# Loads, copies and a bank pool re-arranged at two stage boundaries of a recurrent-attention training kernel

## The chip, the cores and the metric

The kernel runs on one core of one Trainium2 chip. The metric is the device time of one launch in microseconds (us), lower being better. TensorE (PE) multiplies matrices and also transposes 128x128 blocks, VectorE (DVE) and ScalarE (ACT) copy results from PSUM to SBUF and do elementwise work, GpSimd (POOL) does small SBUF copies and issues some transfers, and SyncE (SP) issues most transfers. Each engine works through its own instructions strictly in order.

## The reference, cut to what matters

The output is the forward value and all gradients of `x + A(xn) + B(xn)`, where `xn` is the layer norm of `x` (2048 rows of 512, bf16).

```python
# A: attention over 64 segments of 32 rows; 8 memory rows are carried from segment to segment
for s in range(64):
    h = concat([mem, xn[32*s : 32*s+32]])            # 40 rows
    q, k, v = h @ Wq, h @ Wk, h @ Wv                 # 32 heads of 128
    p = softmax(mask(q @ k.T * 128**-0.5))
    o = (p @ v) @ Wo                                 # summed over heads
    mem, out[s] = o[:8], o[8:]
# B: the dense part
r = relu(xn @ w1 + b1);  B = (r * r) @ w2 + b2       # 512 -> 1792 -> 512
_out, _vjp = jax.vjp(_f, x, mem0, Wq, Wk, Wv, Wo, w1, b1, w2, b2)
return _out, *_vjp(grad_out)
```

## The kernel before, in words

The program has four stages.

1. The first stage (pool `pp`, planner `BIAS_0`) does the layer norm and the dense part in eight blocks of 256 rows. At its start it loads `B_w1` and `B_w2` in seven pieces of 256 KB each (`CUT`), the first blocks of `x` (`ln_in`) and of `grad_out` (`gN0`), and `b1`. It transposes the gradient block (`ps_gT`), the normalised block (`ps_xT`, `ln`) and the weights (`turn_w`: `ps_W2T`, `ps_W1T`) on TensorE, and runs `mlp_a(0)` (`ps_h`), `mlp_b(0)`, and so on.
2. The forward recurrence (pool `pc`, eight PSUM banks `c0` to `c7`) runs `chain(s)` for segments 0 to 63, with work off the chain in between (`l_proj`, `l_attn`, `dw_unit`). At its end `turn` transposes half of Wv on TensorE (`ps_Wv`), and `turn_o` transposes Wo in place inside the tile `WB` (`ps_Wo`): 16 groups of eight 128x128 blocks, each group read back by two copies of 512 elements per partition.
3. The backward recurrence runs `chain(s)` for segments 63 to 0 in a second set of PSUM banks (pool `pc2`, banks `c0` to `c6` and `r0`) and a second set of SBUF tiles (pool `bw`, opened after the forward's pool `fw` is closed). It begins with the remaining 40 groups of transposes of Wv, Wk and Wq (`ps_Wv`, `ps_Wk`, `ps_Wq`) and with the first loads (`l_pre`, `load`). In `chain`, `proj("c", "gO", ...)` multiplies the incoming gradient with the transposed Wo into two banks `ps_gO`, each is copied to a half of the tile `gN` (named `gON` in the profile), and from there transposed again (`ps_gOT`) and multiplied on. `l_pre` does the same for the memory rows (`gL`).
4. The last stage forms the weight gradients of the attention (`ps_gw`).

Within stages 1 to 3 the order of the instructions on every engine is written out by `_Plan.run`. Each piece of work is added with an estimated cost for each engine that may do it and, for a transfer, a time `lat` until it lands. The planner picks greedily by earliest start and by rank, where the rank is the longest estimated path to the end plus a fixed table `BIAS`, and also decides whether DVE or ACT does a copy. The chip does not re-order: if something arrives later than the plan has it, the engine and all that is queued behind it wait. Every `run()` of the kernel before starts from time 0 on all engines and all banks. At the start of the backward's plan a pseudo operation `A({"X": 8.0}, ..., ["WB"])` holds back, in the plan alone, what reads WB.

The Wo rows arrive in an interleaved order, so the old copy in `turn_o` picks every 128th element of PSUM to write a plain row of 128 (`"p j (a c) -> p j a c"` on the SBUF side). Everything behind it sees heads in their natural order.

Of the kernel before, what the change touches and what calls it, by code (L numbers as in the profile page):

```python
# [78 lines left out]
BF16 = mybir.dt.bfloat16  # L79
# [18 lines left out]
def pe(cost, shape, n=8):  # L98
    x = _PE(PE=cost)
    x.shape = shape  # L100
    x.n = n
    return x
# [6 lines left out]
class _Plan:  # L109
# [199 lines left out]
def kernel(  # L309
# [148 lines left out]
    class Stage:  # L458
# [38 lines left out]
        def turn_o(self, kind, nm, reg, key, okey, lift=0.0):  # L497

            for g in range(2 * NI):
                i, d0 = g // 2, 2 * (g % 2)  # L500
                blk = reg.rearrange("p (i c d) -> p i c d", i=NI, c=JQ)[:, i]
                bk = self.bank(kind, [P, 2, JQ, P], BF16, "ps_" + nm)

                def tr(e, blk=blk, bk=bk, d0=d0):
                    for d in range(2):
                        for c in range(JQ):
                            transpose_to(bk()[:, d, c, :], blk[:, c, (d0 + d) * P:(d0 + d + 1) * P])
                self.plan.add(pe(0.46, "f"), tr, [key] if g else [], [bk] + ([] if g else [key]), 1, lift=lift)
                for d in range(2):
                    self.evict(lambda blk=blk, d=d0 + d: blk[:, :, d * P:(d + 1) * P].rearrange("p j (a c) -> p j a c", c=JQ), bk,  # L510
                               lambda bk=bk, d=d: bk()[:, d].rearrange("p c (j a) -> p j a c", j=JQ), [(okey, g, d)], 1, {"DVE": 0.61, "ACT": 0.59})

        def sq_T(self, src, sk, dst, dk, prio):

# [15 lines left out]
        def proj(self, kind, nm, win, wkeys, Wt, col0, dst, prio):  # L530
            for half in range(2):
                bk = self.bank(kind, [P, 512], F32, "ps_" + nm)
                for dq in range(2):
                    def mm(e, half=half, dq=dq, bk=bk):
                        for dc in (2 * dq, 2 * dq + 1):
                            for j in range(JQ):
                                c0 = col0 + j * HW + half * 512
                                nc.tensor.matmul(  # L538
                                    bk()[32 * j:32 * (j + 1), :], lhsT=win(dc), rhs=Wt(dc, c0),
                                    start=(dc == 0), stop=(dc == DC - 1), tile_position=(0, 32 * j),  # L540
                                )
# [37 lines left out]
        def mixed(self, nm, pre, terms, rkeys, dst, prio, lift=0.0):  # L579

            bks = [self.bank("d", [P, 512], F32, "ps_" + nm) for _ in range(2)]
            for half in range(2):
                bk = bks[half]

                def mm0(e, half=half, bk=bk):
                    for k in range(4):
                        for x, (lf, rf) in enumerate(pre):
                            nc.tensor.matmul(bk()[:, k * P:(k + 1) * P], lhsT=lf(4 * half + k), rhs=rf(4 * half + k),  # L588
                                             start=(k == 0 and x == 0), stop=False, skip_group_check=True)
                self.plan.add(pe(0.22 * len(pre), "f", 4 * len(pre)), mm0, rkeys[0](half), [bk], prio, lift=lift)  # L590
            for half in range(2):
                bk = bks[half]

                def mm(e, half=half, bk=bk):
                    for k in range(4):
                        i = 4 * half + k
                        for x, (lf, rf) in enumerate(terms):
                            for j in range(JQ):
# [3 lines left out]
                self.plan.add(pe(0.222 * len(terms), "d", 16 * len(terms)), mm, rkeys[1](half), [bk], prio)  # L602
# [94 lines left out]
    with tc.tile_pool(name="p0", bufs=1) as p0, \  # L697
# [4 lines left out]
        def tl(name, shape, dt=BF16):  # L702
            return p0.tile(shape, dt, name=name)
# [179 lines left out]
        for g in range(NRB):  # L883
            if g == 0:
                ln_in(0)
                for h, (f0, f1) in enumerate(CUT):
                    sg.dma(lambda f0=f0, f1=f1: W1[:, :, P * f0:P * f1],
                           lambda f0=f0, f1=f1: B_w1.rearrange("(c p) f -> p c f", p=P)[:, :, P * f0:P * f1], [], [("W1", h)], lat=6.0)
                    if h == 1:
                        sg.dma(lambda: gN0, lambda: pair(gflat, 0), [], ["gxb"], lat=6.0)  # L890
                        sg.dma(lambda: b1Tb[:], lambda: B_b1.rearrange("(c p) -> p c", p=P), [], ["b1Tb"], lat=5.0)
                    sg.dma(lambda f0=f0, f1=f1: W2[:, f0:f1, :],
                           lambda f0=f0, f1=f1: B_w2.rearrange("(c p) d -> p c d", p=P)[:, f0:f1, :], [], [("W2", h)], lat=8.0)
                sg.dma(lambda: b2r[:], lambda: B_b2.rearrange("(o n) -> o n", o=1), [], ["b2r"], lat=5.0)
                A({"DVE": 0.1}, lambda e: V.tensor_copy(b1T[:], b1Tb[:]), ["b1Tb"], ["b1T"])
                ln(0)
                bk = sg.bank("B", [P, DC, RB], BF16, "ps_gT")

                def trg(e, bk=bk):
                    for k in range(2):  # L900
                        for dc in range(DC):
                            transpose_to(bk()[:, dc, k * P:(k + 1) * P], gN0[:, k, dc * P:(dc + 1) * P])
                A({"PE": 0.5}, trg, ["gxb"], [bk])
                A({"DVE": 0.7, "ACT": 1.05}, lambda e, bk=bk: ev({"DVE": "v", "ACT": "s"}[e], gTb[0], bk()[:]), [bk], [("gT", 0)])
                for u in range(FC // 2):
                    turn_w(u, "W2T")
                ln_in(1)
                ln_in(2)
                ln(1)
# [30 lines left out]
                   lat=8.0, cost=0.6, eng="POOL")  # L940
        plan.run()

    with tc.tile_pool(name="fw", bufs=1) as fw, \
            tc.tile_pool(name="pc", bufs=1, space=bass.MemoryType.PSUM) as pc:
        PLp = []
        for v in range(SPB):
            t_ = fw.tile([P, NI, RL], BF16, name="PLp%d" % v)
# [342 lines left out]
        l_attn(TC - 1)  # L1290
        sg.turn("m", "Wv", Wqkv[2], ("WA", 2), "WvT", 0, 8)
        sg.turn_o("c", "Wo", WB[:], "WB", "WoT", 40.0)
        plan.run()

    bw_cm = tc.tile_pool(name="bw", bufs=1)
    bw = bw_cm.__enter__()
    pc2_cm = tc.tile_pool(name="pc2", bufs=1, space=bass.MemoryType.PSUM)
    pc = pc2_cm.__enter__()
    if True:
        def tl(name, shape, dt=BF16):  # L1300
            return bw.tile(shape, dt, name=name)
# [39 lines left out]

        plan = _Plan(tc, PAR[2], BIAS[2])
        S7 = [("c", x) for x in range(7)]
        sg = Stage(plan, pc, {"c": (4, S7), "f": (1, S7), "l": (1, S7), "e": (1, S7), "w": (4, S7), "r": (1, [("r", 0)]), "d": (3, S7), "t": (3, S7)})
        A = plan.add
        V = nc.vector
        LKIND = "r"
# [248 lines left out]
        for y in range(NEARLY):  # L1596
# [2 lines left out]
                    nc.tensor.matmul(pw0[k]()[:], lhsT=HNc[:, RCS[y], k * P:(k + 1) * P], rhs=gbuf[y][:, 0:512],  # L1599
                                     start=(y == 0), stop=False)  # L1600
            A(pe(0.86, "f", 4), mm0, [("gn", y), ("HN", RCS[y] // BPC), "gNat"], pw0)
        plan.run()
    bw_cm.__exit__(None, None, None)

    with tc.tile_pool(name="p5b", bufs=1) as p5b, tc.tile_pool(name="p5e", bufs=1) as cs1, \
# [60 lines left out]
        with tc.manual_schedule():  # L1666
            load_gn(0)
            for x in range(4 * JQ):
# [4 lines left out]
                if x == 2 * JQ:  # L1673
# [3 lines left out]
                gns = gq.pop(x)  # L1677
                bks = [(lambda b=b: b()[:]) for b in (
                    (pw0 if x == 0 else [sg.bank("w", [P, 512], F32, "ps_gw", b.key) for b in pw0])
                    + [sg.bank("w", [P, 512], F32, "ps_gw", k) for k in S7 + [("r", 0)] if k not in [b.key for b in pw0]])]  # L1680
# [25 lines left out]
    pc2_cm.__exit__(None, None, None)  # L1706
    fww_cm.__exit__(None, None, None)


# [33 lines left out]
```

## Time and profile before

| what | value |
|---|---|
| three timed runs | 2806.7 us median, 2800.26 to 2809.99 |
| profiled execution, first to last instruction | 2798.3 us |
| busy share PE / DVE / ACT / POOL | 95% / 47% / 35% / 29% |
| PE busy in 0 to 30 us | 18.25 us |
| PE busy in 30 to 250 us | 215.52 of 220 us |
| PE busy in 1186 to 1236 us (end of forward, start of backward) | 43.49 of 50 us |
| PE busy in 1236 to 2200 us (backward) | 926.36 of 964 us |

The profiled execution is one launch. Its own time is given only as its span from the first to the last instruction, which is 8.4 us under the median of the timed runs and 2.0 us under the lowest of them. A stage's worth is read from the idle time of TensorE in it. A bracket at the end of a row of the timeline is the time that the engine stood idle before that instruction, and behind the arrow is what ended it.

### The profile page before, as it was taken

Reading aid. Unit: us, or ns where it says so; the run is one execution under the profiler, and the core shown is the slowest. Engines: PE = TensorE matmul, PEld = TensorE weight load, DVE = VectorE, ACT = ScalarE, POOL = GpSimd, SP = SyncE. Lnnn points to the kernel's source line nnn. Section 1 sums busy time; section 2 is a strip of 40 time slices with the busy share of each in tenths; the row PEclk is TensorE's granted clock in tenths of the full one; section 3 lists DMA queues with packets and bytes.
Section 4 is the critical chain, followed back from the end, with each engine's and each line's share of the span. In section 5 each row is a group of like instructions: output and inputs, shape, how many; then the busy total and the mean of one; then the engine's idle time right before and its main releaser. Section 6 shows DMA issues by size and latency. Waiting matters only on the chain.

```text
span 2798.3 us, 125071 instructions
## 1 busy us (share of the span) xinstructions
PE 2664.6 (95%) x54888; PEld 1538.5 (55%) x55072; DVE 1327.3 (47%) x3327; ACT 985.8 (35%) x2012; POOL 824.8 (29%) x2431
## 2 busy tenths in 40 slices
PE   8998999999999999999999999999999899999999
PEld 6664555555555555575555555555555444444444
DVE  5544455555455555565455455555455402232322
ACT  4333444444444444364444444444444300000000
POOL 1111111111111111145555555555555301112210
PEclk9999999999999999999999999999999999999999
DMA  6657656555557566647777676777766698788861
GB/s 211 202 172 205 180 160 175 164 166 163 156 169 186 169 185 175 177 118 178 187 181 187 179 189 179 189 192 190 188 182 177 201 344 273 232 255 270 257 185 42
DMA packets 499792, 530.91 MB, mean 190 GB/s; under 512 B 223845, under 2 KB 325398, under 8 KB 497070
## 3 DMA queue, kind: packets, MB, share of 16 engines
q1 hardware_dynamic: 480254, 463.06, 59.9%
q0 software_dynamic: 15056, 53.56, 5.6%
q8 instruction: 430, 7.05, 1.1%
q10 hardware_dynamic: 3936, 6.29, 0.7%
q14 instruction: 116, 0.95, 0.1%
HBM read 249.77 MB, written 237.52 MB: 174 GB/s over the span
## 4 chain that ended last, share of the span: by engine, by line
PE 45%; DVE 4%; issue 3%; DMA 3%; ACT 1%; POOL 1%; SPq 0%; DVEq 0%; ACTq 0%; POOLq 0%
PE ps_gw L1690 14%; PE ps_dRA L1370 8%; PE ps_gw L1694 5%; PE ps_gO L538 3%; PE ps_dRL L1370 3%; PE ps_d L624 2%; DMA dLN<-S_GNL 2%; PE ps_d L573 1%; PE ps_d L599 1%; PE ps_gOT L429 1%; PE ps_d L588 1%; PE ps_gm L1524 1%; PE ps_gL L538 1%; PE ps_dL L1481 1%; PE ps_dP L1468 1%
## 5 line engine op out<-in xcount | busy, mean ns | idle before, releaser
L1370 PE MATMUL ps_dRA<-WA,dT 128*32 128x512 bf16 x6144 | 377.0, 381 | 5.3 <-issue 2.5
L1690 PE MATMUL ps_gw<-WA,WB 128*128 128x512 bf16 x1505 | 330.6, 379 | 1.6
L1690 PEld LDWEIGHTS <-WB 128*128 128x128 bf16 x1896 | 185.4, 98 | 225.0 <-issue 1.7
L538 PEld LDWEIGHTS <-PA 128*32 128x32 bf16 x8192 | 195.4, 96 | 192.3 <-DVE PA L1190 22.3
L435 ACT CAST dN<-ps_d 128x512 bf16<-128x512 f32 x372 | 207.4, 590 | 184.7 <-PE ps_d L599 112.3
L1370 PEld LDWEIGHTS <-dT 128*32 128x32 bf16 x6144 | 151.8, 96 | 154.2 <-DVE dT L517 17.3
L433 DVE CAST gwo<-ps_gw 128x512 bf16<-128x512 f32 x64 | 40.0, 685 | 399.9 <-PE ps_gw L1690 268.5
L435 ACT CAST gwo<-ps_gw 128x512 bf16<-128x512 f32 x64 | 33.1, 598 | 510.2 <-PE ps_gw L1690 357.3
L517 DVE STREAM_TRANSPOSE dT<-dN 128x256 f32<-128x256 f32 x384 | 165.4, 437 | 72.1 <-ACT dN L435 66.5
L1020 POOL TENSOR_TENSOR P<-P,rsA 128x320 bf16<-128x320 bf16 x64 | 46.2, 722 | 458.8 <-DVE rsA L1015 244.1
L624 PEld LDWEIGHTS <-PB 32*32 32x32 bf16 x8192 | 119.8, 92 | 76.4 <-DVE PB L1168 23.9
L1701 POOL DMA_DIRECT2D out_dram<-gwo x96 | 71.6, 753 | 293.9 <-ACT gwo L435 265.1
L538 PE MATMUL ps_q<-WA,PA 128*32 128x512 bf16 x2048 | 145.2, 382 | 5.5 <-DVE PA L1190 3.7
L1039 PE MATMUL ps_RA<-WB,OT 128*32 128x256 bf16 x4096 | 129.0, 277 | 17.7 <-DVE OT L517 13.6
L538 PE MATMUL ps_k<-WA,PA 128*32 128x512 bf16 x2048 | 144.9, 381 | 0.3 <-DVE PA L1190 0.3
L435 ACT CAST kN<-ps_k 128x512 bf16<-128x512 f32 x125 | 73.4, 587 | 194.1 <-PE ps_k L538 172.2
L538 PE MATMUL ps_v<-WA,PA 128*32 128x512 bf16 x2048 | 140.7, 379 | 0.0
L1039 PEld LDWEIGHTS <-OT 128*32 128x32 bf16 x4096 | 103.9, 98 | 46.2 <-DVE OT L517 32.0
L538 PE MATMUL ps_gO<-WB,PA 128*32 128x512 bf16 x2048 | 126.4, 380 | 1.0 <-DVE PA L1528 1.0
L611 POOL COPY BDL<-bPLL 32x64 bf16<-32x64 bf16 x256 | 60.4, 236 | 218.4 <-PE ps_d L573 210.4
L433 DVE CAST qN<-ps_q 128x512 bf16<-128x512 f32 x62 | 42.9, 692 | 171.5 <-PE ps_q L538 169.5
L1254 PE MATMUL ps_dw<-sx,anT 128*128 128x512 bf16 x339 | 108.2, 384 | 6.6 <-DMA sx<-S_XN 2.8
(315 smaller groups left out, 5300.8 us busy)
## 6 DMA issues: line engine op xcount, KB each, us to landing
S_GN<-dN SPq DMA_DIRECT2D x192, 256.0 KB
WA<-S_GN SPq DMA_DIRECT2D x150, 256.0 KB
S_Q<-qN SPq DMA_DIRECT2D x64, 256.0 KB
S_K<-kN SPq DMA_DIRECT2D x64, 256.0 KB
S_V<-vN SPq DMA_DIRECT2D x64, 256.0 KB
S_ON<-oN SPq DMA_DIRECT2D x64, 256.0 KB
bqN<-S_Q SPq DMA_DIRECT2D x64, 256.0 KB
bkN<-S_K SPq DMA_DIRECT2D x64, 256.0 KB
```

What stands on the lines that cost most here:

```text
L433: nc.vector.tensor_copy(out, in_)
L435: nc.scalar.copy(out, in_)
L517: self.plan.add({"DVE": 0.445}, lambda e, half=half: nc.vector.transpose(words(dst, half).rearrange("p (i c r) -> p i c r", i=4, c=2), src ...
L538: nc.tensor.matmul(bk()[32 * j:32 * (j + 1), :], lhsT=win(dc), rhs=Wt(dc, c0), start=(dc == 0), stop=(dc == DC - 1), tile_position=(0, 32 ...
L611: f(q_(dst, j)[:, :, j, 0:c], q_(src_f(), j))
L624: nc.tensor.matmul(bk()[32 * j:32 * j + m, k * P:(k + 1) * P], lhsT=lf(j, i), rhs=rf(j, i), start=(k == 0 and x == 0), stop=(x == n - 1), ...
L1039: nc.tensor.matmul(bk()[32 * c:32 * (c + 1), :], lhsT=sg.rows(OTt, i, j), rhs=Wo[:, JQ * i + j, dh * DH:(dh + 1) * DH], start=(i == 0 and ...
L1254: nc.tensor.matmul(bks[x]()[:], lhsT=anT[x][:, c, :], rhs=sx[z][:], start=(c == 0), stop=(c == TC - 1))
L1370: nc.tensor.matmul(bk()[32 * j:32 * (j + 1), :], lhsT=sg.rows(XT, i, j), rhs=wtf(t, i, j), start=(first and i == 0), stop=(last and i == N ...
L1690: nc.tensor.matmul(bks[n](), lhsT=HNc[:, rc, dc * P:(dc + 1) * P], rhs=gns[y][:, hf * 512:(hf + 1) * 512], start=(y == 0), stop=(y == NRC ...
L1694: nc.tensor.matmul(bks[n](), lhsT=gns[y][:, k * P:(k + 1) * P], rhs=GOc[:, rc, :], start=(y == 0), stop=(y == NRC - 1))
L1701: nc.gpsimd.dma_start(outWs[t][dc * P:(dc + 1) * P, 4 * hf:4 * hf + 4, j, :], wt[:].rearrange("p (i e) -> p i e", i=4))
```

## The change

There are four parts.

- b1 is loaded as 14 rows of 128 elements into `b1Tb` of 14 partitions, transposed on TensorE through a bank of kind "B" (`ps_b1`) and then copied to `b1T`. Before, it was loaded element by element into 128 partitions and copied.
- In the first stage the planner's figures for the weight pieces and the first gradient block change from a cost of 0.42 with `lat` 6.0 or 8.0 to a cost of 0.85 with `lat` 2.6.
- `turn_o` copies Wo's transposes in runs of 32 elements on both sides, which leaves the 128 columns of a head interleaved; the planner's DVE cost for it goes from 0.61 to 0.37. The copies out of `ps_gO` and `ps_gL` undo the interleaving, by writing 2-byte elements at a distance of four.
- Both recurrences use the one PSUM pool `pc` with its eight banks; `r0` becomes `c7`. The forward's `run()` returns when engines and banks come free, and the backward's `run(state)` starts from that, relative to the last end on PE, DVE and ACT. The pseudo operation on WB goes from 8.0 to 0.5.

`mixed` also gets options (`full`, `inter`, `kind`) which no call uses.

```diff
-    def run(self):
+    def run(self, state=None):
...
-        free, loose, used = {}, {}, {}
+        free, loose = ({k: v - state[2] for k, v in x.items()} for x in state[:2]) if state else ({}, {})
+        used = {}
...
+        return free, loose, max(o.end for o, e in seq if e in ("PE", "DVE", "ACT"))
...   turn_o
-   blk[:, :, d * P:(d + 1) * P].rearrange("p j (a c) -> p j a c", c=JQ), bk,
-   bk()[:, d].rearrange("p c (j a) -> p j a c", j=JQ), ... {"DVE": 0.61, "ACT": 0.59})
+   blk[:, :, d * P:(d + 1) * P].rearrange("p j (c a) -> p j c a", c=JQ), bk,
+   bk()[:, d].rearrange("p c (j a) -> p j c a", j=JQ), ... {"DVE": 0.37, "ACT": 0.59})
...   proj
+                if nm in ("gO", "gL"):
+                    self.evict(lambda half=half: dst[1][:, 4 * half:4 * half + 4, :].rearrange("p i (a c) -> p i c a", c=JQ),
+                               bk, lambda bk=bk: bk()[:].rearrange("p (i c a) -> p i c a", i=4, c=JQ), [(dst[0], half)], prio, EV_F)
+                    continue
...   first stage
-        b1Tb, b1T = tl("b1Tb", [P, FC]), tl("b1T", [P, FC], F32)
+        b1Tb, b1T = tl("b1Tb", [FC, P]), tl("b1T", [P, FC], F32)
-   W1 pieces: lat=6.0            W2 pieces: lat=8.0            gN0: lat=6.0
+   W1, W2 pieces and gN0: lat=2.6, cost=0.85
-   sg.dma(lambda: b1Tb[:], lambda: B_b1.rearrange("(c p) -> p c", p=P), [], ["b1Tb"], lat=5.0)
+   sg.dma(lambda: b1Tb[:], lambda: B_b1.rearrange("(c p) -> c p", p=P), [], ["b1Tb"], lat=5.0)
-                A({"DVE": 0.1}, lambda e: V.tensor_copy(b1T[:], b1Tb[:]), ["b1Tb"], ["b1T"])
+                bb1 = sg.bank("B", [P, FC], BF16, "ps_b1")
+                A({"PE": 0.1}, lambda e: transpose_to(bb1()[:], b1Tb[:]), ["b1Tb"], [bb1])
+                A({"DVE": 0.1}, lambda e: V.tensor_copy(b1T[:], bb1()[:]), [bb1], ["b1T"])
...   between the recurrences
-        plan.run()
+        state = plan.run()
-    pc2_cm = tc.tile_pool(name="pc2", bufs=1, space=bass.MemoryType.PSUM)
-    pc = pc2_cm.__enter__()
-        sg = Stage(plan, pc, {... "r": (1, [("r", 0)]), ...})
+        sg = Stage(plan, pc, {... "r": (1, [("c", 7)]), ...})
-        A({"X": 8.0}, lambda e: None, [], ["WB"])
+        A({"X": 0.5}, lambda e: None, [], ["WB"])
-        plan.run()
+        plan.run(state)
```

More of the change, by code (lines that the diff above doesn't have):

```diff
@@ L509, in turn_o @@
                 for d in range(2):
[L510 to L511 removed]
+                    self.evict(lambda blk=blk, d=d0 + d: blk[:, :, d * P:(d + 1) * P].rearrange("p j (c a) -> p j c a", c=JQ), bk,
+                               lambda bk=bk, d=d: bk()[:, d].rearrange("p c (j a) -> p j c a", j=JQ), [(okey, g, d)], 1, {"DVE": 0.37, "ACT": 0.59})
         def sq_T(self, src, sk, dst, dk, prio):
@@ L577, in blocks, with mixed @@
                            bk, lambda bk=bk: bk()[:], [(dst[0], half)], prio, EV_F)
-        def mixed(self, nm, pre, terms, rkeys, dst, prio, lift=0.0):
-            bks = [self.bank("d", [P, 512], F32, "ps_" + nm) for _ in range(2)]
-            for half in range(2):
+        def mixed(self, nm, pre, terms, rkeys, dst, prio, lift=0.0, full=False, inter=False, kind=None):
+            bks = [self.bank(kind or "d", [P, 512], F32, "ps_" + nm) for _ in range(2)]
+            for half in ((0, 1) if not inter else ()):
                 bk = bks[half]
@@ L592, in mixed, with mm0 @@
                 bk = bks[half]
+                if inter:
+                    def mm0(e, half=half, bk=bk):
+                        for k in range(4):
+                            for x, (lf, rf) in enumerate(pre):
+                                nc.tensor.matmul(bk()[:, k * P:(k + 1) * P], lhsT=lf(4 * half + k), rhs=rf(4 * half + k),
+                                                 start=(k == 0 and x == 0), stop=False, skip_group_check=True)
+                    self.plan.add(pe(0.22 * len(pre), "f", 4 * len(pre)), mm0, rkeys[0](half), [bk], prio, lift=lift)
                 def mm(e, half=half, bk=bk):
@@ L597, in mm @@
                         for x, (lf, rf) in enumerate(terms):
+                            if full:
+                                nc.tensor.matmul(bk()[:, k * P:(k + 1) * P], lhsT=lf(i), rhs=rf(i),
+                                                 start=False, stop=(x == len(terms) - 1), skip_group_check=True)
+                                continue
                             for j in range(JQ):
@@ L601, in mm @@
                                                  skip_group_check=True)
-                self.plan.add(pe(0.222 * len(terms), "d", 16 * len(terms)), mm, rkeys[1](half), [bk], prio)
+                cost = pe(0.22 * len(terms), "f", 4 * len(terms)) if full else pe(0.222 * len(terms), "d", 16 * len(terms))
+                self.plan.add(cost, mm, rkeys[1](half), [bk], prio)
                 self.evict(lambda half=half: dst[1][:, 4 * half:4 * half + 4, :].rearrange("p i e -> p (i e)"),
@@ L941 @@
         plan.run()
-    with tc.tile_pool(name="fw", bufs=1) as fw, \
-            tc.tile_pool(name="pc", bufs=1, space=bass.MemoryType.PSUM) as pc:
+    pc_cm = tc.tile_pool(name="pc", bufs=1, space=bass.MemoryType.PSUM)
+    pc = pc_cm.__enter__()
+    with tc.tile_pool(name="fw", bufs=1) as fw:
         PLp = []
@@ L1679 @@
                     (pw0 if x == 0 else [sg.bank("w", [P, 512], F32, "ps_gw", b.key) for b in pw0])
-                    + [sg.bank("w", [P, 512], F32, "ps_gw", k) for k in S7 + [("r", 0)] if k not in [b.key for b in pw0]])]
+                    + [sg.bank("w", [P, 512], F32, "ps_gw", k) for k in S7 + [("c", 7)] if k not in [b.key for b in pw0]])]
                 kq = [(k % 4) * 2 + k // 4 for k in range(8)] if t < 3 else range(8)
@@ L1705 @@
                     ln_bwd(*z)
-    pc2_cm.__exit__(None, None, None)
+    pc_cm.__exit__(None, None, None)
     fww_cm.__exit__(None, None, None)
```

8 lines of the change are left out of this document (4 added, 4 removed).

## The prediction

> **What bounds the kernel now.** I read the page's totals and its chain first, then busy time by stage.
>
> ```profile
> span 2798.3 us, 125071 instructions
> PE 2664.6 (95%) x54888; PEld 1538.5 (55%) x55072; DVE 1327.3 (47%) x3327; ACT 985.8 (35%) x2012; POOL 824.8 (29%) x2431
> PE 45%; DVE 4%; issue 3%; DMA 3%; ACT 1%; POOL 1%; SPq 0%; DVEq 0%; ACTq 0%; POOLq 0%
> ```
>
> ```profile
> core 0: us, PE busy (x) PEld busy (x) DVE busy (x) ACT busy (x) POOL busy (x), PEclk, DMA share, GB/s
> 0.00:30.00 30.00, 18.25 (x172) 16.38 (x173) 16.79 (x70) 15.81 (x40) 7.13 (x39) 1.00 0.70 190
> 30.00:250.00 220.00, 215.52 (x1775) 140.04 (x1799) 111.75 (x448) 78.25 (x182) 32.43 (x53) 0.99 0.64 201
> 1186.00:1236.00 50.00, 43.49 (x965) 36.75 (x962) 34.93 (x69) 31.07 (x51) 20.89 (x46) 0.97 0.49 130
> 1236.00:2200.00 964.00, 926.36 (x26152) 555.01 (x26148) 504.16 (x1250) 406.58 (x802) 532.44 (x1891) 1.00 0.71 182
> ```
>
> TensorE is the bound: busy 95% of the span and largest on the chain. The change takes no TensorE work away, so it can only win TensorE's idle time, or lose by adding some. Idle lies in the first 30 us (11.75), around the boundary of the recurrences (6.5 of 50) and thinly in the backward (37.6 of 964). From 30 to 250 us TensorE is 98% busy, so what is won at the start is kept.
>
> **The start: why TensorE idles.** The timeline, start and duration first:
>
> ```profile
> 3.76 0.63 ACT L759 ACTIVATE maskL<-xN 128x512 bf16<-128x512 bf16 x1 [1.52 <-DMA xN<-in_A_x_dram]
> 4.31 1.02 SPq L479 DMA_DIRECT2D WB<-in_B_w_dram  x2
> 7.72 0.60 SPq L479 DMA_DIRECT2D xN<-in_A_x_dram  x1
> 8.07 0.15 DVE L769 TENSOR_SCALAR var_t<-var_t 128x1 f32<-128x1 f32 x1 [0.40 <-ACT maskL L767]
> 8.37 0.60 SPq L479 DMA_DIRECT2D b1Tb<-in_B_b_dram  x1
> 13.48 0.63 ACT L759 ACTIVATE maskL<-xN 128x512 bf16<-128x512 bf16 x1 [5.44 <-DMA xN<-in_A_x_dram]
> 14.11 0.19 ACT L772 ACTIVATE sdev<-var_t 128x1 f32<-128x1 f32 x1
> 9.29 2.77 PE L429 MATMUL ps_W2T<-ident,W 128*128 128x128 bf16 x24
> 15.14 1.01 PE L429 MATMUL ps_W2T<-ident,W 128*128 128x128 bf16 x8 [3.08 <-DVE WB L433]
> 15.95 0.63 PE L429 MATMUL ps_xT<-ident,WB 128*128 128x128 bf16 x4
> 16.37 1.06 PE L429 MATMUL ps_W2T<-ident,W 128*128 128x128 bf16 x8
> 17.33 0.68 DVE L783 COPY PA<-ps_xT 128x1024 bf16<-128x1024 bf16 x1
> 18.06 1.87 PE L797 MATMUL ps_h<-PA,WB 128*128 128x256 bf16 x8 [0.63 <-DVE mean_t L761]
> ```
>
> Three windows of one us:
>
> ```profile
> 10.00:11.00 1.00, 1.00 (x13) 1.00 (x11) 0.00 (x0) 0.00 (x0) 0.00 (x0) 1.00 1.09 344
> 12.00:13.00 1.00, 0.06 (x1) 0.00 (x0) 0.00 (x0) 0.00 (x0) 0.00 (x0) 1.00 0.48 23
> 13.00:14.00 1.00, 0.00 (x0) 0.00 (x0) 0.00 (x0) 0.52 (x1) 0.00 (x0) 1.00 0.36 81
> ```
>
> The variance of block 0's second half is ready at 8.2, but its square root runs at 14.11: ACT has the second block's first pass ahead of it, and that waits 5.44 us for x, issued at 7.72 behind ten pieces. From the root hang the last ps_xT, the copy to PA and the first ps_h at 18.06, whose W1 piece had been issued at 4.31. At 344 GB/s a piece takes 262 KB/344 = 0.76 us; the old plan counted 0.42.
>
> **Part 1, b1 by rows, and part 2, the order.** With 0.85 a piece the planner expects the second block's x at 0.42 + 10 x 0.85 + 0.42 + 3.5 = 12.8 us, where the chip had 13.48, so it has reason to put the root and the copies of ps_W2T ahead of that pass. The root then runs at 8.3. From root to first ps_h the old order took 18.06 - 14.11 = 3.95, other copies in between, so ps_h comes near 12.2, 5.8 earlier. But by 18.06 five groups of ps_W2T, eight blocks each, were done (24 + 8 + 8), and by 12.2 I count three, as the four banks allow; the two others (8 x 0.056 us each, the warm spacing used below for ps_Wq) return 0.9, leaving 4.9. If no copy comes in between it is up to 1.5 more: 6.4. The least is 0, if the order does not change. I take 5.2, the wait of 5.44 less 0.2 for b1's transpose, since that wait is the row of what goes.
>
> The b1 load of 1792 single elements is what I read into the two slow microseconds, 23 and 81 GB/s beside 344: (1 - 23/344) + (1 - 81/344) = 1.7 us of transfer time, hidden behind the wait for x. Its cover goes with that wait, but the load goes too; 14 rows still cost an issue (0.60). The new transpose makes TensorE wait for b1, with ps_W2T and ps_h queued behind it: each microsecond that b1 lands late would come off the 5.2. It also takes a "B" bank, so that the second ps_W2T group waits for b1's copy. SP's other issues only change places: the gradient block and the second x against the pieces. What is late next is W1: its third piece, the thirteenth transfer, lands at about 3.76 + 12 x 0.76 = 12.9 (an estimate from the first landing) and is wanted two blocks of ps_h after 12.2, so it hides.
>
> **The boundary.** The groups by form first, then timeline, chain (start, duration) and one window:
>
> ```profile
> L435 ACT COPY WB<-ps_Wo 128x512 bf16<-128x512 bf16 x17 | 8.8, 604 | 3.3 <-DVE WB L433 3.1 <-PE ps_Wo L429 0.2
> L433 DVE COPY WB<-ps_Wo 128x512 bf16<-128x512 bf16 x15 | 9.2, 685 | 3.5 <-ACT WB L435 3.4
> L433 DVE COPY KT<-ps_kT 128x512 bf16<-128x512 bf16 x124 | 47.3, 420 | 0.4 <-PE ps_kT L429 0.4
> ```
>
> ```profile
> 1209.14 6.06 PE L429 MATMUL ps_Wo<-ident,WB 128*128 128x128 bf16 x104
> 1215.68 0.32 SPq L479 DMA_DIRECT2D bkLN<-S_KL  x1
> 1215.85 1.80 PE L429 MATMUL ps_Wo<-ident,WB 128*128 128x128 bf16 x24 [0.65 <-DVE WB L433]
> 1221.74 2.44 PE L429 MATMUL ps_Wq<-ident,WA 128*128 128x128 bf16 x24 [4.08 <-ACT WB L435]
> 1226.18 0.40 POOL L1441 COPY bVT<-VTL 128x256 bf16<-128x256 bf16 x1 [1.38 <-DMA VTL<-S_VL]
> ```
>
> ```profile
> 1224.18 2.03 PE ps_Wk L429 x24
> 1226.21 0.45 PE ps_Wq L429 x8
> ```
>
> ```profile
> 1222.00:1223.00 1.00, 1.00 (x14) 1.00 (x12) 0.44 (x1) 0.00 (x0) 1.00 (x2) 0.54 0.50 114
> ```
>
> **Part 3, Wo's copies.** 17 x 0.604 and 15 x 0.685 fill both engines for 10.3 us; TensorE delivers the 128 transposes in about 128 x 0.056 = 7.2. In runs of 32 the nearest row is KT, also written in runs of 32: 0.420. Both engines together then take 32/(1/0.604 + 1/0.420) = 7.9 us, 2.4 less.
>
> **Part 4, one pool.** The first ps_Wq waits 4.08 us until the last copy of Wo has left the old pool. With one pool it waits for its own bank, so this and the 0.65 go: 4.7. The gap had a second price: granted clock 0.54, and 48 transposes in 2.44 + 2.03 = 4.5 us where warm ones take 48 x 0.056 = 2.7. That is 1.8 more; together 6.5, of which 7.9 - 7.2 = 0.7 stays as copies still behind TensorE. I take 5.8. Part 3 has no second gain: its copies stood in the same gap. What is late next are the loads. SP's first for the backward comes at 1215.68, held by the closing of the SBUF pool, which stays; VT is filled by POOL only at 1226.18. The new plan starts from SP's earlier free time and knows nothing of that hold, and X at 0.5 lets gO come early. If gO starts near 1219, its product, cast, transpose and copy take it to 1223 (an estimate: 1.9, 0.6, 0.4 and 0.4 us, plus hand-overs), and if the transposes of Wq, Wk and Wv are put too far behind, TensorE waits there for VT, with the whole backward queued behind it: up to 1226.6 - 1223 = 3.6 us. So the gain lies between 5.8 - 3.6 = 2.2 and 6.5. POOL's first copies wait for the same loads and move with them; SP's loads keep their place behind the pool's closing.
>
> The Trainium skill, "TensorE: Matmul & The Clock Gate", Part 1, says that the cold phase comes after an idle window of some 3.4 us and that its length varies with the phase of a free-running window, so that a fixed count of cold matmuls should not be fitted. By it the 1.8 is an estimate; the row agrees that a 4.08 us gap is enough, and without that term the boundary would give 4.0.
>
> **Part 3's other side: the copy of gO.**
>
> ```profile
> L435 ACT CAST gON<-ps_gO 128x512 bf16<-128x512 f32 x127 | 74.4, 586 | 98.1 <-PE ps_gO L538 98.1
> 1276.93 0.59 ACT L435 CAST gON<-ps_gO 128x512 bf16<-128x512 f32 x1 [0.28 <-PE ps_gO L538]
> 1277.57 0.23 PEld L429 LDWEIGHTS <-gON 128*128 128x128 bf16 x4
> ```
>
> The cast ends at 1277.52 and its reader loads at 1277.57: no slack. Two casts a step, 64 steps, now write at a distance of 8 bytes. No row shows ACT writing so. Fewer elements it does not write, so no gain; the near bound is ACT's copy with a scattered read, 604 against 586: 18 ns x 128 = 2.3 us. The far one is what the scattered form cost DVE, 685 - 420 = 265 ns: 17 us with one cast a step on the path. ACT is the engine here, so I take 6 ns, 0.8 us.
>
> The Trainium skill, "SBUF — State Buffer", Door 1, puts SBUF lines at 16 bytes and calls strides up to 8 bf16 elements free, needing two hits a line: by it the price is nil and the sum 0.8 lower. But two is what this stride leaves, the very limit; no run here shows it.
>
> **Re-ordering.** The forward's order should hold but for its end. The backward's starts from other times and is drawn anew. Its tables give one value for each kind of work, the same in all 64 steps, so nothing speaks for a gain or a loss; a fifth of the 37.6 us idle either way is my bound, 7.5. I take 0.
>
> **Sum.** -5.2 - 5.8 + 0.8 = -10.2: a span of 2788.1. The profiled span stands 8.4 under the median, so the median goes from 2806.7 to 2796.5, 0.36% faster. A measurement can tell about 0.3%, 8.4 us, from no change.
>
> **The rivals.**
> Half of it (0.25): one wait moves instead of going, to x in another place at the start or to VT at the boundary. For it: the plan's start knows nothing of the pool's hold. Against: 31 groups of transposes, 14 us, lie ready as filling. -5.2 - 2.2 + 0.8 gives 2800.1; with the start lost, -5.8 + 0.8 gives 2801.7.
> More (0.12): the new backward order also wins idle time: 2796.5 - 7.5 = 2789.0.
> The order costs (0.08), slower: TensorE waits more often for a dT, maskA or load that the plan has early, once a step. With -10.2 won it ends slower than 8.4 from 18.6/64 = 0.29 us a step; at 0.32 the time is 2817.
> Strided casts (0.06), slower: at the far bound on both casts, 128 x 0.265 = 34 us, so 2806.7 - 11 + 34 = 2830; it decides from 0.15 us a cast. Against: ACT's scattered read cost it only 18 ns.
>
> **How the numbers follow.** The forecast has 0.49 and by itself reaches from 2790 to 2800, past the bound at 2806.7 - 8.4 = 2798.3 with its slow edge, 0.03. Faster is 0.49 + 0.12 - 0.03 = 0.58; within is 0.25 + 0.03 = 0.28; slower 0.08 + 0.06 = 0.14. The range leaves out the two slower rivals and the best corner: low is 2806.7 - 6.5 - 6.5 - 7.5 = 2786; high is the half case with 7.5 lost, 2808.
>
> **What would show it.** Start: the square root before the second block's pass, ps_h near 11 to 13 us, no second of 23 GB/s. Boundary: ps_Wo on DVE near 420 ns, no wait of over 1 us before the first ps_Wq, no clock of 0.5. Backward: gON casts 586 to 604 ns; idle in the 964 us within 30 to 45. Wrong if gON is longer by over 0.1 us, if a dP waits for VT, or if that idle passes 50.

## The result, and the profile after

The changed kernel is slower: 2828.89 us median (2825.6 to 2833.31, six runs) against 2805.77 us for the kernel before (six runs too), a ratio of 1.0086 with a 95% interval of 1.0070 to 1.0102. The forecast was 2796.5 us. The profiled execution took 2833.31 us, with a span 33.2 us longer than that of before. The medians differ by only 23.1 us: the traced execution is the slowest of its six here, and by its span near the fastest before.

The page's totals of the changed kernel, span and busy time of each engine:

```profile
span 2831.5 us, 125257 instructions
PE 2680.4 (95%) x55073; PEld 1535.9 (54%) x55073; DVE 1329.0 (47%) x3332; ACT 1074.2 (38%) x2007; POOL 825.1 (29%) x2431
```

DVE and POOL are busy as long as before; ACT is busy 88 us longer with five instructions fewer. So some of its instructions have become dearer. Busy time by stage, the same stretches as in the prediction:

```profile
core 0: us, PE busy (x) PEld busy (x) DVE busy (x) ACT busy (x) POOL busy (x), PEclk, DMA share, GB/s
0.00:30.00 30.00, 21.26 (x225) 19.37 (x226) 21.24 (x84) 18.18 (x45) 7.04 (x39) 1.00 0.75 220
30.00:250.00 220.00, 216.06 (x1820) 137.99 (x1819) 109.20 (x435) 78.37 (x182) 32.49 (x53) 1.00 0.64 202
1186.00:1236.00 50.00, 43.33 (x934) 36.67 (x930) 31.81 (x74) 28.96 (x46) 20.94 (x46) 0.93 0.48 127
1236.00:2200.00 964.00, 896.65 (x25264) 532.79 (x25256) 490.34 (x1206) 477.81 (x771) 511.36 (x1814) 1.00 0.68 176
```

TensorE's idle time fell by 3.0 us in the first 30 us, stayed the same at the boundary, and rose in the backward from 37.6 to 67.4 us of 964. The first and last copy of ps_mem mark the first and last step of the forward, those of ps_gm the first and last of the backward. In the timeline of before:

```profile
249.62 0.19 DVE L1190 CAST PA<-ps_mem 128x32 bf16<-128x32 f32 x1 [0.33 <-PE ps_mem L1185]
...
1188.89 0.19 DVE L1190 CAST PA<-ps_mem 128x32 bf16<-128x32 f32 x1 [0.62 <-PE ps_mem L1185]
1259.83 0.19 DVE L1528 CAST PA<-ps_gm 128x32 bf16<-128x32 f32 x1
...
2209.31 0.19 DVE L1528 CAST PA<-ps_gm 128x32 bf16<-128x32 f32 x1 [0.44 <-PE ps_gm L1524]
```

and of after:

```profile
244.67 0.19 DVE L1211 CAST PA<-ps_mem 128x32 bf16<-128x32 f32 x1 [0.33 <-PE ps_mem L1206]
...
1187.82 0.19 DVE L1211 CAST PA<-ps_mem 128x32 bf16<-128x32 f32 x1 [0.61 <-PE ps_mem L1206]
1260.58 0.19 DVE L1547 CAST PA<-ps_gm 128x32 bf16<-128x32 f32 x1
2243.52 0.19 DVE L1547 CAST PA<-ps_gm 128x32 bf16<-128x32 f32 x1 [0.44 <-PE ps_gm L1543]
```

So the balance runs: 4.95 us ahead as the forward begins, 1.1 ahead at its last step, 0.75 behind after the boundary, 34.2 behind at the end of the backward. The backward's 62 intervals cost 982.9 us for 949.5, or 0.54 us more each. That is at the upper end, since the trace of before has the shortest backward of all versions with plain casts: the eight of them lie between 949.5 and 954.7 us, and against their mean of 952.1 it is 0.50 us.

Groups by form in the changed kernel (count, busy, mean ns, idle before them), and TensorE's wait for the first of them from 1236 to 2236 us (total, times, longest):

```profile
L437 ACT CAST gON<-ps_gO 128x512 bf16<-128x512 f32 x127 | 159.3, 1356 | 71.8 <-PE ps_gO L540 71.4
L437 ACT CAST gLN<-ps_gL 128x512 bf16<-128x512 f32 x32 | 42.1, 1326 | 41.1 <-PE ps_gL L540 41.1
```

```profile
PE ps_gOT L431 <- ACT gON L437: 40.2, 68, 0.9
```

The same wait in the kernel before:

```profile
PE ps_gOT L429 <- ACT gON L435: 0.6, 2, 0.4
```

The strided cast takes 1356 ns where the plain one took 586, and TensorE's wait for it has become the largest new row of the backward.

### The profile page after: what moved, and what is told of

It reads as the page before. It is cut to its first block, busy times and chain, and to the rows that moved or that the text cites. A ratio compares the mean times of both kernels' runs of the same rounds, so it can differ in the third digit from the quotient of the medians.

```text
span 2831.5 us, 125257 instructions
## 1 busy us (share of the span) xinstructions
PE 2680.4 (95%) x55073; PEld 1535.9 (54%) x55073; DVE 1329.0 (47%) x3332; ACT 1074.2 (38%) x2007; POOL 825.1 (29%) x2431
## 5 line engine op out<-in xcount | busy, mean ns | idle before, releaser
L437 ACT CAST gON<-ps_gO 128x512 bf16<-128x512 f32 x127 | 159.3, 1356 | 71.8 <-PE ps_gO L540 71.4
L1275 PE MATMUL ps_dw<-sx,anT 128*128 128x512 bf16 x448 | 123.0, 385 | 4.6 <-DMA sx<-S_XN 4.6
```

Source lines behind the costliest of these rows:

```text
L437: nc.scalar.copy(out, in_)
L1275: nc.tensor.matmul(bks[x]()[:], lhsT=anT[x][:, c, :], rhs=sx[z][:], start=(c == 0), stop=(c == TC - 1))
```

## The experiments

Each run has its own runs of the kernel before beside it, with medians of 2804.9 to 2805.5 us; a ratio of 0.001 is 2.8 us. Positions of single steps come from one profiled execution each, and executions of one kernel lie up to 22 us apart (2793.60 to 2815.96 us for b1 by rows alone).

**The cast alone, its writes made plain.** The changed kernel, reading PSUM at a distance of 32 elements and writing a plain row:

```diff
-  dst....rearrange("p i (a c) -> p i c a", c=JQ),  bk()[:].rearrange("p (i c a) -> p i c a", i=4, c=JQ)
+  dst....rearrange("p i (a c) -> p i a c", c=JQ),  bk()[:].rearrange("p (i c a) -> p i a c", i=4, c=JQ)
```

> The changed kernel with one edit: the copies out of ps_gO and ps_gL read PSUM at a distance of 32 elements and write a plain row, in place of reading a plain row and writing 2-byte elements at a distance of 4. Theory A (the write at a distance is the whole loss): the gON copies fall from 1290-1431 ns to 586-610, TensorE's waits for gON in the backward fall from 40.2 us to under 3, and the time falls by about 63 steps x 0.54 = 34 us of the changed profile's 2831.5, less the spread between single runs: median 2795 to 2804, ratio to before 0.996 to 1.000. Theory B (the new order at the boundary, or the shared pool, costs every step): the copies get shorter but the time stays above 2815. Theory C (any scattered access costs the same): the copies stay near 1300 ns and so does the time, near 2829.

Measured: 2798.43 us, ratio 0.9979 (0.9967 to 0.9991). Its group of casts:

```profile
L437 ACT CAST gON<-ps_gO 128x512 bf16<-128x512 f32 x127 | 74.3, 585 | 100.2 <-PE ps_gO L540 100.2
```

The same elements move in the same order of work, the cast is back at 585 ns, and TensorE's wait for it is back at 0.6 us. Theory A holds: the whole loss, 0.0107 or 30 us, hangs on which side carries the scatter.

**Part 3 undone, and part 3 alone.** The first is the changed kernel with the old copies of Wo and plain casts; the second is the kernel before with only these lines:

```diff
-  blk[...].rearrange("p j (a c) -> p j a c", c=JQ),  bk()[:, d].rearrange("p c (j a) -> p j a c", j=JQ),  {"DVE": 0.61, ...}
+  blk[...].rearrange("p j (c a) -> p j c a", c=JQ),  bk()[:, d].rearrange("p c (j a) -> p j c a", j=JQ),  {"DVE": 0.37, ...}
+  if nm in ("gO", "gL"): ...   # the strided cast
```

> The changed kernel with part 3 undone: Wo's transposes copied as before (DVE cost 0.61), gO and gL copied plainly. Parts 1, 2 and 4 stay. Theory A: gON copies 586 ns, median 2797 to 2806 (ratio 0.997 to 1.000): the start is 5 us earlier, and the boundary wins little since DVE waits for the loads there. Theory B: above 2815. Against e1 it says what the faster Wo copies are worth: nothing if DVE's wait at the boundary ends at the same time, up to 2.4 us if not.

> The kernel before with part 3 alone: Wo's transposes copied in runs of 32, gO and gL copied with the write at a distance of 4. Theory A: gON copies 1290 to 1430 ns, 63 steps x 0.54 us = 34 us longer, median 2834 to 2842, ratio 1.010 to 1.013. Theory B: within 5 us of before.

Measured: without part 3 2797.51 us, ratio 0.9966 (0.9953 to 0.9979); part 3 alone 2831.04 us, ratio 1.0083 (1.0066 to 1.0099). Without part 3 the time is as theory A has it, and it is no worse than with the scattered read: next to the other parts, Wo's faster copies win nothing that shows. Part 3 alone reproduces the loss, and its trace loses 30.4 us between the first and the last step of the backward; it stays under the 2834 to 2842 expected, as it also wins 3.9 us at the boundary (below), which the expectation left out. A new order of the backward is not needed for the loss.

**The copies by themselves.** A kernel of nothing but copies of 512 elements per partition, four of each form, first on ACT and then on DVE, with one engine at work at a time (in the strided f32 rows a GpSimd copy runs beside part of them):

```diff
+  flat = w[:, 0:512];  st = lambda n: w[:, 0:512 * n].rearrange("p (k s) -> p s k", s=n)[:, 0]
+  act(flat, ps[:])  # four times, then dve; then st(2), st(4), st(8), st(32), the kernel's own pattern, pairs, runs of 32, a scattered read
```

> No part of the computation but copies of 512 elements per partition, one engine at a time, four of each form, on ACT and DVE from a float32 bank (and on POOL from SBUF); the outputs are not formed. Forms: plain; bf16 written at a distance of 2, 4, 8, 32 elements; the changed kernel's own pattern; pairs of bf16 at a distance of 4 pairs; runs of 32; the read scattered at 32 elements with a plain write; float32 written at a distance of 1, 2, 4. Theory A1 (lone 2-byte writes are the price, whatever the distance): distance 2, 4 and 8 all near 1300 ns, pairs and all float32 forms at the plain 586 (ACT) and 691 (DVE). Theory A2 (the price is by lines touched, and grows with distance): distance 2 near 800, 4 near 1300, 8 and more higher still, pairs and float32 at the same distance in bytes as high. Theory D (contention with other engines in the full kernel): all forms at 586 and 691 when alone. Scattered read: 586 to 610 on ACT.

Measured, ACT's rows of the timeline. The seven CAST rows are, in order: plain, distance 2, 4, 8 (elements of 2 bytes), the kernel's pattern, pairs of elements 16 bytes apart, scattered read; the two COPY rows write f32 at a distance of 8 and 16 bytes:

```profile
14.30 2.44 ACT L58 CAST w<-ps 128x512 bf16<-128x512 f32 x4 [12.28 <-DVE ps L55]
19.66 3.00 ACT L58 CAST w<-ps 128x512 bf16<-128x512 f32 x4 [2.93 <-DVE w L61]
25.73 5.25 ACT L58 CAST w<-ps 128x512 bf16<-128x512 f32 x4 [3.07 <-DVE w L61]
36.32 9.77 ACT L58 CAST w<-ps 128x512 bf16<-128x512 f32 x4 [5.33 <-DVE w L61]
...
75.21 5.25 ACT L58 CAST w<-ps 128x512 bf16<-128x512 f32 x4 [9.68 <-DVE w L61]
85.79 2.52 ACT L58 CAST w<-ps 128x512 bf16<-128x512 f32 x4 [5.33 <-DVE w L61]
...
96.61 2.44 ACT L58 CAST w<-ps 128x512 bf16<-128x512 f32 x4 [2.93 <-DVE w L61]
...
108.73 2.54 ACT L58 COPY wf<-ps 128x512 f32<-128x512 f32 x4 [2.64 <-DVE wf L61]
...
114.65 4.36 ACT L58 COPY wf<-ps 128x512 f32<-128x512 f32 x4
```

and DVE's for distance 4 and 8:

```profile
31.02 5.26 DVE L61 CAST w<-ps 128x512 bf16<-128x512 f32 x4 [5.32 <-ACT w L58]
46.12 9.78 DVE L61 CAST w<-ps 128x512 bf16<-128x512 f32 x4 [9.84 <-ACT w L58]
```

A quarter of each is one copy: 0.61 us plain, 0.75, 1.31 and 2.44 us at 4, 8 and 16 bytes; at a distance of 32 elements ACT's row was 9.60, no dearer than at 8. The kernel's own pattern takes 5.25 / 4 = 1.31 us with nothing else running, the price seen in the kernel. So neither contention nor the engine is at fault: DVE pays the same to 0.01 us at these distances. What costs is the write of lone 2-byte elements, the more the further apart, up to 16 bytes; pairs 16 bytes apart cost nothing (0.63), and a read scattered by 128 bytes in PSUM costs nothing. No expectation holds whole. A1 had the pairs right but one price for all distances, and f32 elements at 16 bytes cost 1.09 us after all; A2 had the growth with the distance right, but the pairs wrong; D is refuted. Why the price grows so is open.

**One half only.** The changed kernel with the first half's casts strided and the second's plain, and the reverse. The plain half's columns stay in the old order, so the products behind them are left unreordered.

```diff
-  if nm in ("gO", "gL"):
+  if nm in ("gO", "gL") and half == 0:     # in the other kernel: half == 1
```

> The changed kernel with only the first half's casts of gO and gL strided; those of the second half are written plainly, so their columns stay in the old order and the products behind them are left unreordered. Theory: the two casts of a step stand one behind the other on ScalarE, and each delays the transposes that read it, but TensorE can fill behind the first with the products of the other half; the loss is the last one's, so half the strided casts give less than half of the 30 us between the changed kernel and the scattered read: 2798 to 2810. Rival: the loss goes by ScalarE's time (160 casts by 0.74 us, 118 us, of which 30 us reach the end), and half the casts give half of it, 2813, whichever half. A third possibility, the first cast being the one that holds TensorE: 2820 or more.

> The changed kernel with only the second half's casts of gO and gL strided, those of the first written plainly and their columns left in the old order. Theory (the last cast holds the path): 2815 to 2828, most of the changed kernel's loss. Rival (by ScalarE's time): 2813. If the first cast is what holds TensorE: 2798 to 2805.

Measured: first half 2821.98 us, ratio 1.0063 (1.0048 to 1.0078); second half 2816.88 us, 1.0051 (1.0031 to 1.0071). Against the scattered read (0.9979) that is 24 and 20 us, where both halves cost 30. The two cannot be told apart, and by the medians each alone costs more than half. The first kernel fits the possibility that the first cast holds TensorE (2820 or more), the second fits the theory that the last one does (2815 to 2828), and each refutes the other. The proportional rule's 2813 lies under both intervals, for the second by less than 1 us. A pair of casts in the timeline of the first kernel (x2: both in one row):

```profile
1538.83 1.73 ACT L437 CAST gON<-ps_gO 128x512 bf16<-128x512 f32 x2 [0.93 <-PE ps_gO L540]
```

of the second:

```profile
1538.59 0.58 ACT L437 CAST gON<-ps_gO 128x512 bf16<-128x512 f32 x1 [0.93 <-PE ps_gO L540]
1539.45 1.30 ACT L437 CAST gON<-ps_gO 128x512 bf16<-128x512 f32 x1 [0.28 <-PE ps_gO L540]
```

and of the changed kernel:

```profile
1529.31 2.56 ACT L437 CAST gON<-ps_gO 128x512 bf16<-128x512 f32 x2
```

Plain, the pair takes 0.58 + 0.28 + 0.58 = 1.44 us, with a gap for ps_gO in the middle. A dear first cast fills that gap, so the pair ends 0.3 us later, but its own transposes wait 0.7; a dear second one ends 0.7 later; both end 1.1 later. Against the trace of before a step became 0.30, 0.33 and 0.54 us longer, against the mean of the versions with plain casts 0.26, 0.29 and 0.50. The delays lie partly beside each other and beside TensorE's other work, so 160 casts that are 0.74 to 0.77 us dearer, 122 us by their durations, put 30 us on the end.

**The start alone.** The kernel before with parts 1 and 2.

```diff
+  ... B_w1 ... lat=2.6, cost=0.85        # and the other pieces
+  ... b1Tb [FC, P], "(c p) -> c p", transpose into ps_b1
```

> The kernel before with the start of the change alone: b1 by rows with its transpose, and the transfers' times of 2.6 and 0.85 us that draw the first stage's order anew. The changed kernel had its first ps_h 2.96 us earlier than before (15.10 for 18.06) and its first ps_mem 4.95 us earlier. Theory: the start wins 4.9 us and all of it reaches the end: median about 2801, ratio near 0.9983, ps_mem and ps_gm steps earlier by 4 to 5 us throughout. Rival: the forward gives it back, as the changed kernel lost 3.3 us in its sixth step where a load is awaited: then the steps from the sixth on stand only 1 to 2 us earlier and the median is 2804 or more.

Measured: 2801.92 us, ratio 0.9983 (0.9970 to 0.9996), first ps_h at 15.08. The theory holds in the median, and the start does win its 4.9 us within the interval of 1 to 8. Its single trace fits neither the theory's 4 to 5 us throughout nor the rival's 1 to 2 from the sixth step on: it stands 4.4 us ahead at the first ps_mem, 6.1 at the sixth, 2.1 at the last, and 3.1 behind at the last ps_gm, in stages whose code is that of before. So how much the forward gives back it cannot say.

**b1 by rows alone.** Part 1 without part 2.

```diff
-  b1Tb [P, FC],  B_b1.rearrange("(c p) -> p c", p=P)
+  b1Tb [FC, P],  B_b1.rearrange("(c p) -> c p", p=P),  transposed on TensorE
```

> The kernel before with b1 loaded by rows and transposed, the planner's transfer times as they were. Theory: the order of ScalarE stays, with the square root behind the second block's first pass, so that only the slow transfer of single elements goes: x's second block lands 1.5 to 2 us earlier than 13.48, the first ps_h likewise, and the time falls by 0 to 2 us (2804 to 2806). Rival: the load of b1 was the whole of the start's gain, with ps_h near 15.1 and the time at about 2801.

Measured: 2803.37 us, ratio 0.9994 (0.9978 to 1.0010), no difference. Both expectations of the mechanism missed:

```profile
8.70 0.37 SPq L479 DMA_DIRECT2D xN<-in_A_x_dram  x1
14.33 0.63 ACT L759 ACTIVATE maskL<-xN 128x512 bf16<-128x512 bf16 x1 [6.35 <-DMA xN<-in_A_x_dram]
```

The transfers run at 303 to 336 GB/s from 10 to 14 us, the hole is gone, and still x comes 0.85 us later than the 13.48 of before, and the first ps_h comes at 19.08. x was issued at 8.70 for 7.72, as b1's load now goes ahead of it, at 4.83, with an issue of 1.27 us. In two other versions with the start of before x came at 13.80 and 14.05, so part of the 0.85 is the difference between executions, but nothing was won. So the slow transfer was hidden, and the start's gain comes with the new order; the new order without b1 by rows was not run.

**The shared pool alone.** The kernel before with part 4.

```diff
-  pc2 = tc.tile_pool(...);  plan.run();             A({"X": 8.0}, ...)
+  one pool pc;              plan.run(state);        A({"X": 0.5}, ...)
```

> The kernel before with the shared PSUM pool, the plan's state handed on and X at 0.5, nothing else: Wo's copies and the casts of gO stay in plain order. Theory: the 4.08 us wait of the first ps_Wq becomes one for its own bank, under 1.5 us, and the backward begins about 3.5 us earlier (the difference that the version without Wo's copies showed at the boundary); median about 2802. Rival: the wait only moves to VectorE's zeroing of gT behind the loads, as in the changed kernel, where the boundary's net was near 0: ps_gm's first step within 1 us of before, median 2805 to 2807.

Measured: 2802.53 us, ratio 0.9992 (0.9977 to 1.0006). The wait of 4.08 us and the cold clock behind it are gone: eight transposes of ps_Wq run at once, and the next wait 0.61 us:

```profile
1223.90 1.09 PE L431 MATMUL ps_Wq<-ident,WA 128*128 128x128 bf16 x16 [0.61 <-ACT WB L437]
```

Clock 1.00 in all 50 us, and the step from the last ps_mem to the first ps_gm 3.4 us shorter than before. The trace agrees with the theory, though it needs the other traces beside it (below); the time, by its interval, with anything from 6 us won to 2 lost.

**The zeroing of gT on GpSimd.** The version with the scattered read, and:

```diff
-  A({"DVE": 0.1}, lambda e: V.memset(gT[pl][...], 0.0), ...)
+  A({"POOL": 0.1}, lambda e: nc.gpsimd.memset(gT[pl][...], 0.0), ...)
```

> The version with the scattered read, and the zeroing of gT's last rows at the end of the backward's preparation moved from VectorE to GpSimd. Theory: VectorE's in-order wait of about 6 us in front of the copy of ps_Wv was for that zeroing alone, which waits for GpSimd's copy of gL behind the loads; without it the 5.8 us wait of ps_Wk goes, and the end comes 3 to 5 us earlier than with the scattered read alone: median 2793 to 2796. Rival: the loads themselves hold the first gO and dP, TensorE's filling only runs out at another place, and the first ps_gm and the time stay within 1 us of the scattered read's (2798).

Measured: 2796.07 us, ratio 0.9964 (0.9951 to 0.9977). TensorE's 5.85 us in front of ps_Wk go, but 3.35 come back one place later:

```profile
1232.61 2.75 PE L540 MATMUL ps_gO<-WB,PA 128*32 128x512 bf16 x24 [3.35 <-POOL PA L1577]
```

So the wait was DVE's, for the zeroing, as the theory had it, and TensorE's filling runs out at another place, as the rival had it: the first ps_gO waits for the zeroing itself, which now stands behind GpSimd's copies, and behind this gap the granted clock is at 0.57 again. The median lies just above the theory's 2793 to 2796. Against the scattered read alone (0.9979) the intervals overlap: a gain of 4 us is likely, not shown.

**Both gains without part 3.** Part 3 undone, and the zeroing on GpSimd.

> The changed kernel without Wo's copies in runs of 32 (2797.5) and with the zeroing of gT's last rows on GpSimd. Theory: the new order of the start, the shared pool and the moved zeroing add up; the scattered read went from 2798.4 to 2796.1 with that move, so here some 2 us come off as well: 2794 to 2797. Rival: without Wo's faster copies there was no wait behind the zeroing to take away (the largest of TensorE's waits there was 1.3 us), and the time stays within 1 us of 2797.5.

Measured: 2798.12 us, ratio 0.9978 (0.9964 to 0.9992), by its median the rival's, though the interval holds the theory's 2794 to 2797 too. The trace decides: from the last ps_mem to the first ps_gm it takes 67.5 us, and the version without the move 67.4, so there was no such wait left. Five versions thus beat both kernels (this one, the two with the scattered read, the one without part 3, and the start alone), at 0.9964 to 0.9983, and cannot be told apart. The lowest figure is that with the scattered read and the zeroing on GpSimd.

## Why the prediction was wrong, point by point

**The failed step is the price of the strided cast.** It was taken as 6 ns with a far bound of 265 ns; it is 740 to 770 ns. Both bounds were rows of scattered reads (ACT's 604 for 586, DVE's 685 for 420), and the change scatters the write. "No row shows ACT writing so" was true, and that should have made the bound wider. The rival "Strided casts" had the place right, and 2830 us came out by luck: it multiplied a price three times too small with a path on which every cast counts in full, where 30 of 122 us count. By the threshold it gave, 0.15 us a cast, the 30 / 128 = 0.23 that reached the end decides.

The Trainium skill, "SBUF — State Buffer", Door 1, calls strides up to 8 bf16 elements free; the rows above differ, with 1.31 us at 4 and 2.44 us at 8 against 0.61, and they decide.

**The start was right in size, in part for another reason.** The timeline of after:

```profile
6.76 1.03 PE L431 MATMUL ps_W2T<-ident,W 128*128 128x128 bf16 x8 [6.76 <-DMA W<-in_B_w_dram]
...
7.83 0.69 DVE L435 COPY WB<-ps_W2T 128x1024 bf16<-128x1024 bf16 x1 [2.14 <-PE ps_W2T L431]
...
9.46 0.20 ACT L790 ACTIVATE sdev<-var_t 128x1 f32<-128x1 f32 x1 [2.91 <-DVE var_t L787]
...
14.37 0.68 DVE L801 COPY PA<-ps_xT 128x1024 bf16<-128x1024 bf16 x1
14.50 0.62 PE L431 MATMUL ps_W1T<-ident,WB 128*128 128x128 bf16 x8 [0.36 <-DMA W<-in_B_w_dram]
15.10 1.03 PE L815 MATMUL ps_h<-PA,WB 128*128 128x256 bf16 x8
```

The wait of 5.44 us for x is gone, as forecast. The root runs at 9.46 and not 8.3, because the variance on DVE now stands behind the first copy of ps_W2T, which waits for the weights, and that of ps_gT; from there to ps_h it is 5.6 us, not 3.95. So ps_h is at 15.10 instead of near 12.2. But by then five groups of weights are transposed (four of ps_W2T, one of ps_W1T), as many as before at 18.06, and not three. The second ps_W2T group does wait for b1's copy, 0.80 us, where 0.2 was counted for b1. The first ps_mem came 4.95 us earlier, and the start alone 4.8 us (1 to 8) by its ratio, for the 5.2 forecast. The slow load of b1 as a hidden cost, and its disappearance, were right.

**At the boundary the wait moved.** Wo's copies were as forecast (groups by form in the changed kernel, 1200 to 1236 us), 7.3 us of TensorE's transposes with no gap before ps_Wq:

```profile
L431 PE MATMUL ps_Wo<-ident,WB 128*128 128x128 bf16 x128 | 7.3, 219 | 0.0
L435 DVE COPY WB<-ps_Wo 128x512 bf16<-128x512 bf16 x20 | 6.9, 413 | 2.0 <-PE ps_Wo L431 1.9
```

Then, in the timeline:

```profile
1215.22 1.50 PE L431 MATMUL ps_Wq<-ident,WA 128*128 128x128 bf16 x24
...
1224.89 0.23 POOL L629 COPY BPK<-bP 32x64 bf16<-32x64 bf16 x1 [1.08 <-DMA bP<-S_P]
...
1226.87 0.29 POOL L1411 COPY PB<-PA 128x128 bf16<-128x128 bf16 x1
1227.22 0.67 DVE L435 COPY WA<-ps_Wv 128x1024 bf16<-128x1024 bf16 x1 [6.48 <-issue]
1227.23 0.07 DVE L1577 MEMSET PA<- 128x16 uint32 x1
...
1227.94 1.01 PE L431 MATMUL ps_Wk<-ident,WA 128*128 128x128 bf16 x8 [4.96 <-DVE WA L435]
```

and GpSimd in the timeline of before:

```profile
1219.17 0.32 POOL L1336 MEMSET BSLK<- 128x256 bf16 x1
1219.55 0.29 POOL L1392 COPY PB<-PA 128x128 bf16<-128x128 bf16 x1
```

DVE reaches its zeroing of gT early and stands there until GpSimd has copied gL (L1411, the row PB<-PA). The profile puts the 6.48 us to the copy beside the zeroing and names no cause; the version with the zeroing on GpSimd shows whose wait it was. That copy of gL was the first after GpSimd's memsets before, 30.7 us behind the last ps_mem; now it stands behind twelve copies for VT, bPLL and bP and their loads, at 39.1 us, though the load that it needs was issued earlier (1213.88 for 1216.05). DVE's copies of the transposed weights stand behind the zeroing, the banks fill, and TensorE waits 4.96 us; and after the gap it is cold again: 8 transposes in 1.01 us, where 24 took 1.50 before it, at a granted clock of 0.50 from 1227 to 1233 us. The 4.08 us went and 4.96 came, and with them the second price. By the Trainium skill, "TensorE: Matmul & The Clock Gate", Part 1, an idle window of some 3.4 us is enough for that; this trace agrees with its 4.96. This is the rival "Half of it" in part: a wait moved instead of going, though it is at the zeroing and not at VT. The forecast took 5.8 us, 2.2 at least; the traces show nothing won. From the last ps_mem to the first ps_gm they take 70.9 to 72.1 us with the boundary of before (three versions), 70.7 to 72.8 with the pool and Wo's new copies together (four, the changed kernel the longest), and 67.1 to 67.5 with only one of the two (four). Each half of the gain is there alone, 3.4 us with the pool and 3.9 with Wo's copies, and they do not add. With the pool alone the copy of gL is as late, but TensorE, held by Wo's copies, has filling up to there; with both, the filling ends 35.2 us behind the last ps_mem, before the zeroing at 39.4.

**The re-ordering came on GpSimd, not on TensorE.** TensorE's instructions stand in the same order in both traces but for the first stage, so for TensorE "drawn anew" did not come true. GpSimd's copy of gL did change its place, in every version with the shared pool and in none without it, and with Wo's new copies beside it this is the wait above; the prediction took 0 for the re-ordering. "POOL's first copies wait for the same loads and move with them" was wrong here. No run puts this copy back to its old place, so what that would win is open. The forward's loss of 3.9 us of the start's gain is in one trace and not in that of the scattered read (4.4 ahead at its first step, 4.1 at its last). The forward took 936.7 to 942.4 us in the traces with the old start and 939.0 to 944.1 in those with the new one, so I leave it as variation of single executions; a loss of a us or two is not excluded.

Together: start -4.8, boundary about zero, casts +30, by ratios -5.9 + 30 = +24, and +24 was measured (0.0086).

## What to carry to other kernels

Look at which side of a copy carries the scatter: here the same permutation was free as a read from PSUM and 0.74 us dearer as lone 2-byte writes 8 bytes apart. Where no row shows an operation, the nearest row must be near in kind (a write for a write), or the far bound is not a bound; a kernel of such copies alone answers it in one run. An in-order engine that reaches a trivial instruction early (a 0.07 us zeroing) hands its wait to all that is queued behind it. When a plan is drawn from new starting times, compare the order on every engine, the idle ones too: here one small copy on GpSimd, 8 us later than before, took back what the boundary had won.

## What the runs showed of the hardware

Writes of single 2-byte elements from PSUM to SBUF take 2.44 us for 512 elements per partition at 16 bytes apart and no more beyond, 1.31 us at 8 bytes, 0.75 at 4, against 0.61 plain, on ACT; DVE took the same at 4 bytes and beyond. Writes of 4 bytes are cheaper: pairs at 16 bytes cost nothing more, f32 elements cost nothing at 8 bytes (2.54 / 4 = 0.64 us) and 1.09 us at 16. A scattered read is not free in every case: the cast from f32, reading at 128 bytes, took 585 ns for 586, but DVE's bf16 copy of Wo's transposes took 685 ns when it read every 128th element (256 bytes apart) and 413 ns in runs of 32; on ACT the two were 604 and 592 ns.
